# The filter's first layer: products in quarters of the array, and the decay split into a row table, scaled weights, a relu scale and a copy scale

## The chip, the core and the metric

The kernel runs on one core of one Trainium2 chip. The metric is the device time of one execution in microseconds. A profiled execution of the kernel before shows what each engine did; its rows are quoted below.

## What is computed

Three blocks follow one another on a sequence of 12480 positions with 128 channels, all in float32. The change touches only the filter of the first one, which is `h_filt` below.

```python
def _attn_ref(x, v, pos_emb, w1, w2):
    h_mlp = np.maximum(pos_emb @ w1, 0.0) @ w2          # (S,64) @ (64,64), then (S,64) @ (64,128)
    window = np.exp(-0.01 * np.arange(S))[:, None]
    h_filt = h_mlp * window
    u = x * v
    Uf = np.fft.rfft(u, n=2 * S, axis=1); Hf = np.fft.rfft(h_filt, n=2 * S, axis=0)
    y = np.fft.irfft(Uf * Hf[None], n=2 * S, axis=1)[:, :S, :]
    return x * y
# then relu(x @ w_in) ** 2 @ w_out, then elu(x @ w2_in) @ w2_out, with 2048 inner columns each
```

## The kernel before

The transform is a long one split into short ones. A position is 127*n + 63 plus or minus p, with n the row (R = 99 rows) and p = 0..63 the distance from a centre. `phase1` makes the first stage of both transforms, `phase2` the second stage, the product and the way back, and `phase3` the two wide layers, where nearly all of the time goes. The stages hand on through the same engines, so work of one stage starts once the last of the stage before has been issued and its inputs are there.

`phase1` runs in this order, which is also the order in each engine's queue. The kernel writes the order out by hand; TensorE (PE), VectorE (DVE), ScalarE (ACT) and GpSimd (POOL) each take their own instructions strictly in it.

1. `warm` issues six products of zeros on PE. SP, the queue of the loads, has issued the position embedding `post` (3.2 MB in six transfers, `load_pos`), then the tables `t1` and `tq`, then `x` and `v` by `load_xv(j)`, 512 KB each. ACT's queue has issued the table `wz` (the decay window `win` and `w1` twice on the diagonal of a 128x128 block).
2. Eight steps `zstep(s)` make the filter's first layer. In each, eight products (L293) multiply 128 rows of `post` (two sets of 64 features) by the block `w1`. The results lie in two PSUM tiles. The one of c=0 is brought out by ACT in eight instructions of 64 columns each (L302: relu, scaled with the decay of row and tap, which is a value of each partition). The one of c=1 is brought out by DVE in one instruction (L296: maximum with 0, times the window). Both go into a buffer `fb[s % 2]`, of which there are two. Then their sum is made by POOL and their difference by DVE (L309), and both go to `fold`. In the last step DVE makes both.
3. `warm` again, then 16 groups `s1` on the filter (L340): eight products each with the table `t1`, the stationary side being `fold`; ACT copies the result out. DVE meanwhile makes `u = x*v` and folds it (`ufold(j)`: L319, then L322 and L174; for six of the sixteen j twice the folding).
4. 32 groups `s1` on u, two for each j (L340, or L335 for the folded j, whose products each use a quarter of the array, 50 partitions by 64 columns). Their results go over the buffers of `v` (`xu`), which is why the first of them waits for the `ufold`s that read there. After the groups of j the loads of j+NX are issued and `ufold(j+NX)` follows.

`stile` hands out the PSUM tiles of all these steps in turn, four of them until call number NS1. NX is the count of `x` buffers (11), NV the count of separate `v` buffers (3); the `v` of j below 8 go to `xu`.

Of the kernel before, what the change touches and what calls it, by code (L numbers as in the profile page):

```python
# [10 lines left out]
F32 = mybir.dt.float32  # L11
# [3 lines left out]
AF = mybir.ActivationFunctionType  # L15
# [5 lines left out]
S = 12480  # L21
# [27 lines left out]
TOP = float(np.array(0x47EFFFFF, np.uint32).view(np.float32))  # L49
LO0 = 8  # L50
LAG1 = 2
NX = 11
NV = 3
NWARM = 6
NS1 = 55
MID = R // 2
RM = R - MID
FOLDED = (8, 9, 10, 12, 13, 14)
# [35 lines left out]
def tables():  # L94
    n1 = np.arange(R)
    k1 = np.arange(K1)
    k2 = np.arange(N2)
    pe, po = np.arange(CEN + 1), np.arange(1, CEN + 1)
    t = {}
    th = _angle((n1[:, None] - MID) * k1[None, :], N1)  # L100
    tq = np.stack([np.cos(th), -np.sin(th), -np.cos(th)], axis=1)[MID:].reshape(RM, 3 * K1)
    t["tq"] = np.zeros((128, 3 * K1))
    t["tq"][:RM] = t["tq"][64:64 + RM] = tq
    t["t1"] = np.stack([np.cos(th), -np.sin(th), -np.cos(th)], axis=2).reshape(R, 3 * K1)
    tf = np.zeros((2 * NP, N2, N2))
    k = k1[:, None, None] + N1 * k2[None, None, :]
    tf[:K1, :CEN + 1] = np.cos(_angle(pe[None, :, None] * k, L))
    tf[:K1, 0] = 0.5
    tf[:K1, CEN + 1:] = np.sin(_angle(po[None, :, None] * k, L))
    t["tf"] = np.zeros((NP, 128, 2 * N2))  # L110
    t["tf"][:, :N2] = tf.reshape(NP, 2, N2, N2).swapaxes(1, 2).reshape(NP, N2, 2 * N2)
    th = _angle(k2[:, None] * pe[None, :], N2)
    g = np.zeros((128, 128))
    g[:N2, 0] = 1.0
    g[:N2, 1:N2:2] = np.cos(th)[:, 1:]
    g[:N2, 2:N2:2] = np.sin(th)[:, 1:]
    t["g"] = g
    tl = _tiles()
    order = [s * p for p, s in tl[0][3]]
    at = np.concatenate(_rows()) - CEN - 2 * MID * N2  # L120
    c = np.where(k1 == 0, 1.0, 2.0)[:, None] / L
    th = _angle(k1[:, None] * at[None, :], L)
    re, im = c * np.cos(th), -c * np.sin(th)
    n = sum(tl[0][2])
    t["t3"] = np.stack([re[:, :n].reshape(K1, SIZES[0], -1), im[:, :n].reshape(K1, SIZES[0], -1)], axis=2)
    t["t3"] = t["t3"].reshape(K1, -1)
    t["ta"] = np.concatenate([re, im[:KA]])
    side = np.concatenate([np.full(nr, s) for _, _, nrs, rows in tl for (p, s), nr in zip(rows, nrs)])
    t["tb"] = np.concatenate([np.where(side == s, im[KA:], 0.0) for s in (1, -1)])
    sg = np.ones((128, 3))  # L130
    sg[:K1, 0] = sg[K1:, 1] = sg[K1 - KA:, 2] = -1.0
    t["sg"] = sg
    th = _angle((k[2 * PD:, 0, :, None, None] *
                 (np.array(order)[:, None] + N2 * (n1[None, :R - 1] - 2 * MID))[None, None]), L).reshape(KD, N2, -1)
    t["t4"] = np.zeros((128, 2 * th[:, 0].size))
    t["t4"][:N2] = (2.0 / L * np.stack([np.cos(th), -np.sin(th)], axis=1)).transpose(2, 0, 1, 3).reshape(N2, -1)
    pos = _taps().astype(np.float32)
    ok = (pos >= 0) & (pos < S)
    win = np.where(ok, np.exp(np.float32(-0.01) * np.where(ok, pos, np.float32(0.0))), 0.0)
    win = win.transpose(2, 0, 1).reshape(R, 8, 2, 4, 2).transpose(0, 1, 2, 4, 3).reshape(R, 128)  # L140
    t["wz"] = np.concatenate([win, np.zeros((128 - R, 128))])
    return {k: np.ascontiguousarray(a, dtype=np.float32) for k, a in t.items()}


# [19 lines left out]
class Build:  # L164
# [40 lines left out]
    def front(self):  # L205
        ctx0 = self.ctx
        with ExitStack() as self.ctx:
            self.mid = self.pool("mid")
            self.t1 = self.mid.tile([R, K1, 3], F32, name="t1")
            self.tq = self.mid.tile([128, 3, K1], F32, name="tq")  # L210
            self.psb = []
            self.right = ExitStack()
            self.x0pool = ctx0.enter_context(ExitStack())
            self.phase1()
            self.phase2()
            self.right.close()
        self.ctx = ctx0
# [7 lines left out]
    def phase1(self):  # L225
        nc, a = self.nc, self.a
        with ExitStack() as ctx1:
# [19 lines left out]
            self.xt = self.mid.tile([128, KTAIL * 2 * D], F32, name="xt")  # L247
            self.p2 = self.pool("p2")
            xvp = self.right.enter_context(self.tc.tile_pool(name="xv", bufs=1, side="right"))
            win, w1 = self.xt[:R, :128].rearrange("p (s c h n) -> p s c h n", s=8, c=2, h=2), self.xt[:, 128:256]  # L250
            fb = [self.xt[:R, o:o + 1024].rearrange("p (c h n e) -> p c h n e", c=2, h=2, e=E) for o in (256, 1280)]
            post = self.xr[:, :64 * R].rearrange("p (s w) -> p s w", s=8)
            fold = self.xu[2][:R, :2 * C1 * E].rearrange("p (o n e) -> p o n e", o=2, e=E)

# [4 lines left out]

            def load_xv(j):  # L260
                for i, (d, nm, n) in enumerate(((xs, "xc", NX), (vs, "vc", NV))):
                    if i and j < 8:
                        t = self.xu[j // 4][:, 1024 * (j % 4):1024 * (j % 4) + 1024]
                    else:
                        t = xvp.tile([128, 1024], F32, tag=nm, name=nm, bufs=n)
                    d[j] = t
                    nc.sync.dma_start(out=t, in_=a["xv"][j, i])
# [3 lines left out]
                for _ in range(n):  # L271
                    nc.tensor.matmul(ps[:, 0, :128], lhsT=self.zero, rhs=self.zero, start=True, stop=True)

            nc.scalar.dma_start(out=self.xt[:, :256], in_=a["wz"])
            self.copy(self.ebias[:, 2:3], self.zero[:, 0:1])
            for w in range(2):
                load_pos(0, 1, slice(4 * R * w, 4 * R * w + 4 * R))
            warm(NWARM)
            for b, e in ((1, 2), (2, 4), (4, 6), (6, 8)):
                load_pos(b, e)  # L280
            nc.sync.dma_start(out=self.t1.rearrange("p k a -> p (k a)"), in_=a["t1"])
            nc.sync.dma_start(out=self.tq.rearrange("p a k -> p (a k)"), in_=a["tq"])
            for j in range(8):
                load_xv(j)

            def zstep(s):
                f = fb[s % 2]
                for c in range(2):
                    ps = stile(2, 512)[:R, 0]
                    z = ps.rearrange("p (h n e) -> p h n e", h=2, e=E)  # L290
                    for q in range(4):
                        i = 4 * c + q
                        nc.tensor.matmul(ps[:, 128 * q:128 * q + 128], lhsT=post[:, s, i * R:i * R + R], rhs=w1,  # L293
                                         start=(q == 0), stop=(q == 3))
                    if c == 1:
                        nc.vector.scalar_tensor_tensor(  # L296
                            out=f[:, 1], in0=z, scalar=0.0,
                            in1=win[:, s, 1].unsqueeze(3).to_broadcast([R, 2, 4, E]), op0=ALU.max, op1=ALU.mult)
                        continue
                    for h in range(2):  # L300
                        for n in range(4):
                            nc.scalar.activation(out=f[:, 0, h, n], in_=z[:, h, n], func=AF.Relu,  # L302
                                                 scale=win[:, s, 0, h, n:n + 1])
                f = f.rearrange("p c h n e -> p c h (n e)")
                parts = [(nc.gpsimd, 0, slice(0, 2)), (nc.vector, 1, slice(0, 2))]
                if s == 7:
                    parts = [(nc.vector, 0, slice(0, 2)), (nc.vector, 1, slice(0, 2))]
                for eng, o, c in parts:
                    eng.tensor_tensor(out=fold[:, o, 8 * s:8 * s + 8].rearrange("p (c n) e -> p c (n e)", c=2)[:, c],  # L309
                                      in0=f[:, c, 0], in1=f[:, c, 1], op=(ALU.add, ALU.subtract)[o])  # L310

            for s in range(8):
                zstep(s)
# [8 lines left out]
                    nc.vector.tensor_tensor(out=o[:, :, 0], in0=i[:, :, 0], in1=i[:, :, 1], op=ALU.add)  # L322
                    self.sub(nc.vector, o[:, :, 1], i[:, :, 0], i[:, :, 1])

            def s1(i, fb, dst, w, last=None):
                ps = stile(2, 512)
                pv = ps[:, :, :4 * K1].rearrange("p b (c e) -> p b c e", e=2)
                halves = ((0, C1), (C1, N2))
# [8 lines left out]
                                                 start=(j == 0), stop=(j == 3))  # L337
                for j in range(4 if isinstance(fb, list) else 0):
                    for q, (b, e) in enumerate(halves):
                        nc.tensor.matmul(pv[b:e, j // 2, :, j % 2], lhsT=fb[j][q], rhs=self.t1[:, :, q:q + 2],  # L340
                                         start=(j % 2 == 0), stop=(j % 2 == 1))
                b = 0
                for o, n in dst:
                    o = o.rearrange("p (c d) -> p c d", d=w)[:N2, :, 4 * i:4 * i + 4]
                    o, z = o.rearrange("p c (b e) -> p c b e", e=2), pv[:N2, :, b:b + n].rearrange("p b c e -> p c b e")
                    b += n
                    if last and b == 2 * K1:
                        last(o, z)
                    else:
                        self.copy(o, z)  # L350

            for j in range(8, NX):
                load_xv(j)
# [1 line left out]
            for j in range(NX):  # L355
                ufold(j)
            for i in range(E // 4):
                s1(i, [(fold[:, 0, :, 4 * i + c], fold[:, 1, 1:, 4 * i + c]) for c in range(4)], [(self.xr, 2 * K1)], E)
            dst = [(t, n) for t, n in zip(self.xu + [self.xt], (32, 32, 64, 2 * KTAIL))]
            self.raw = {}  # L360
            for j in range(D // 8):
# [674 lines left out]
```

## Time and profile before

| | us |
|---|---|
| median of 3 runs | 1343.35 |
| lowest, highest | 1343.01, 1344.01 |
| profiled execution, its own time | 1345.65 |
| profiled execution, its span (first to last instruction) | 1343.9 |
| PE busy in the span | 1332.8 |

The page of the profile gives the span, the busy time of each engine and the chain of work that ended last. Beneath it lie views of any stretch: instructions in order of time, groups by line and shape, busy time by stretch, the waits. A row of the timeline reads: start, length, engine, line, operation, output<-input, shape, how many instructions were merged into it, and in brackets the idle time before it with what ended that. PE's products in float32 show two records each in the trace, and so do the loads of their weights.

### The profile page before, as it was taken

The page shows a single profiled execution, that of the slowest core. Times are in us where ns is not written, and L with a number is a line of the kernel's source. Part 1 is how long each engine was busy: PE and PEld are TensorE (multiplying, and loading weights), DVE is VectorE, ACT ScalarE, POOL GpSimd, SP SyncE. Part 2 cuts the span into 40 slices and gives each one's busy share as a digit, 9 for nine tenths or more (in the row PEclk, how much of TensorE's full clock was granted, in tenths as well). Part 3 has the DMA queues.
Part 4 walks back from the last instruction along what each step waited for, and adds up shares of the span by engine and source line. Part 5 has one row for each costly group of instructions (what it writes and reads, how often), then busy time and mean ns, then how long its engine had stood idle before and what let it go on. Part 6 is the DMA issues. An engine that isn't in the chain of part 4 may idle for free.

```text
span 1343.9 us, 19149 instructions
## 1 busy us (share of the span) xinstructions
PE 1332.8 (99%) x7150; PEld 1110.1 (83%) x7150; DVE 1182.5 (88%) x1210; ACT 1117.1 (83%) x1431; POOL 621.7 (46%) x364
## 2 busy tenths in 40 slices
PE   9999999999999999999999999999999999999998
PEld 9977778888888888888888888888888888888886
DVE  6969886889989898989899889989898989899897
ACT  6778775788988898889888888988898889888886
POOL 3038680545744454444444444444444445444432
PEclk9999999999999999999999999999999999999999
DMA  9746775301110111011001101110111011100000
GB/s 362 276 134 212 206 233 153 115 1 51 53 49 5 53 53 44 10 53 53 26 28 53 53 9 45 53 52 1 53 53 48 5 53 53 32 5 9 8 8 14
DMA packets 72443, 93.32 MB, mean 69 GB/s; under 512 B 5627, under 2 KB 62966, under 8 KB 72350
## 3 DMA queue, kind: packets, MB, share of 16 engines
q1 hardware_dynamic: 72062, 91.80, 21.9%
q8 instruction: 56, 0.92, 0.3%
q14 instruction: 37, 0.30, 0.1%
q10 hardware_dynamic: 288, 0.30, 0.1%
HBM read 73.72 MB, written 18.32 MB: 68 GB/s over the span
## 4 chain that ended last, share of the span: by engine, by line
PE 96%; DVE 2%; ACT 1%; issue 0%; DMA 0%; POOL 0%; SPq 0%; DVEq 0%; ACTq 0%
PE h L202 39%; PE y L202 38%; PE s L340 3%; PE v L559 3%; PE u L536 3%; PE h L677 2%; PE h L408 2%; PE h L681 2%; PE rt L395 1%; PE s L293 1%; DVE g L956 0%; DVE tn L942 0%; PE s L335 0%; DVE ex L872 0%; PE y L815 0%
## 5 line engine op out<-in xcount | busy, mean ns | idle before, releaser
L174 POOL TENSOR_TENSOR lo<-g,hi 128x1024 fp32r<-128x1024 f32 (+2 forms) x192 | 467.8, 2437 | 602.2 <-DVE tn L942 495.9
L202 PE MATMUL h<-xh,m 128*128 128x512 f32 (+3 forms) x1600 | 421.4, 385 | 3.4 <-DVE g L956 2.3
L202 PE MATMUL y<-hi,m 128*128 128x512 f32 (+2 forms) x1568 | 418.9, 389 | 0.0
L202 PEld LDWEIGHTS h<-xh,m 128*128 128x128 f32 x1600 | 298.6, 188 | 62.6 <-DVE g L956 3.4
L202 PEld LDWEIGHTS y<-hi,m 128*128 128x128 f32 x1568 | 290.0, 188 | 59.5 <-ACT ys L177 4.7
L942 DVE SCALAR_TENSOR_TENSOR tn<-ex,tn 128x1024 f32<-128x1024 f32 (+4 forms) x201 | 240.5, 1196 | 98.0 <-ACT ex L866 96.8
L865 ACT ACTIVATE tn<-h 128x1024 f32<-128x1024 f32 (+4 forms) x201 | 201.7, 1003 | 148.0 <-PE h L202 148.0
L174 DVE TENSOR_TENSOR lo<-ex,hi 128x1024 fp32r<-128x1024 f32 (+3 forms) x192 | 248.5, 1294 | 0.0
L956 DVE SCALAR_TENSOR_TENSOR g<-h,r 128x1024 f32<-128x1024 f32 (+3 forms) x200 | 238.4, 1192 | 9.2 <-ACT r L952 9.2
L202 PE MATMUL h<-xl,m 128*128 128x512 f32 (+3 forms) x800 | 242.2, 384 | 0.0
L202 PE MATMUL y<-lo,m 128*128 128x512 f32 (+2 forms) x784 | 239.8, 387 | 0.8 <-DVE lo L174 0.4
L872 DVE SCALAR_TENSOR_TENSOR ex<-tn,h 128x1024 f32<-128x1024 f32 (+4 forms) x201 | 237.2, 1180 | 1.5
L965 ACT ACTIVATE hi<-r 128x1024 fp32r<-128x1024 f32 (+3 forms) x200 | 209.8, 1049 | 0.5
L952 ACT ACTIVATE r<-h 128x1024 f32<-128x1024 f32 (+3 forms) x200 | 202.4, 1012 | 8.3 <-PE h L202 6.9
L177 ACT ACTIVATE hi<-ex 128x1024 fp32r<-128x1024 f32 (+2 forms) x192 | 203.9, 1062 | 1.6 <-DVE ex L872 1.5
L866 ACT ACTIVATE ex<-h 128x1024 f32<-128x1024 f32 (+4 forms) x201 | 199.8, 994 | 0.0
L202 PEld LDWEIGHTS y<-lo,m 128*128 128x128 f32 x784 | 146.7, 188 | 32.0 <-DVE lo L174 2.4
L202 PEld LDWEIGHTS h<-xl,m 128*128 128x128 f32 x800 | 149.6, 188 | 28.5
L551 POOL TENSOR_TENSOR pt<-pt 127x256 f32<-127x256 f32 x43 | 33.5, 779 | 82.0 <-DVE pt L548 81.9
L559 PE MATMUL v<-pt,g 127*128 127x512 f32 (+1 forms) x92 | 48.5, 612 | 0.0
L756 DVE SCALAR_TENSOR_TENSOR v<-z,sg 118x384 f32<-118x384 f32 (+3 forms) x75 | 43.0, 574 | 0.0
L548 DVE TENSOR_TENSOR pt<-u,hh 127x512 f32<-127x512 f32 (+1 forms) x46 | 31.2, 679 | 13.0 <-PE u L536 12.5
(93 smaller groups left out, 1059.0 us busy)
## 6 DMA issues: line engine op xcount, KB each, us to landing
Zd<-z SPq DMA_DIRECT2D x45, 256.0 KB
z<-Zd SPq DMA_DIRECT2D x48, 192.0 KB
xc<-in_xv_dram SPq DMA_DIRECT2D x16, 512.0 KB
z<-Zd SPq DMA_DIRECT2D x48, 136.5 KB
tb<-in_tf_dram SPq DMA_DIRECT2D x46, 127.0 KB
out_dram<-ys SPq DMA_DIRECT2D x22, 256.0 KB
m<-in_xv_dram SPq DMA_DIRECT2D x8, 512.0 KB
vc<-in_xv_dram SPq DMA_DIRECT2D x8, 512.0 KB
```

The source lines that it names most:

```text
L174: return eng.tensor_tensor(out=out, in0=a, in1=b, op=ALU.subtract)
L177: self.nc.scalar.activation(out=out, in_=in_, func=AF.Copy)
L202: self.nc.tensor.matmul(outs[b], lhsT=w[:, b, h], rhs=x[b], start=first and i in ((0,) if one else (0, 2)), stop=last and i in ((5,) if on ...
L559: nc.tensor.matmul(v, lhsT=self.g[:N2], rhs=pt.rearrange("p j r d -> p (j r d)"), start=True, stop=True)
L756: nc.vector.scalar_tensor_tensor(out=v[:k, i, q], in0=zi[:, :, 1], scalar=self.sg[:k, i:i + 1], in1=zi[:, :, 0], op0=ALU.mult, op1=ALU.add)
L865: nc.scalar.activation(out=e["tn"][:, b], in_=e["h"][:, b], func=AF.Tanh, scale=0.5)
L866: nc.scalar.activation(out=e["ex"][:, b], in_=e["h"][:, b], func=AF.Exp)
L872: nc.vector.scalar_tensor_tensor(out=e["g"][:, b], in0=e["em"][:, b], scalar=0.0, in1=e["h"][:, b], op0=ALU.min, op1=ALU.max)
L942: after = nc.vector.scalar_tensor_tensor(out=pa["em"][:, b], in0=pa["ex"][:, b], scalar=1.0, in1=pa["tn"][:, b], op0=ALU.add, op1=ALU.mult)
L952: nc.scalar.activation(out=f["r"], in_=f["h"], func=AF.Relu)
L956: nc.vector.scalar_tensor_tensor(out=f["g"], in0=f["h"], scalar=0.0, in1=f["r"], op0=ALU.max, op1=ALU.mult)
L965: nc.scalar.activation(out=f["hi"], in_=f["r"], func=AF.Square)
```

## The change

The first layer's products are cut into quarters. A step covers eight taps on both sides of the centre. `post` is laid out so that partitions 0 to 63 hold its first four taps and 64 to 127 its last four; each product takes 64 of these partitions, 64 (or the last 35) of the 99 rows, and 64 columns of weights. A step has 32 such products in place of eight, and its results fill both banks of one PSUM tile: z[:, 0] and z[:, 1] are the two sides, whose sum and difference are wanted. The decay exp(-0.01*pos) is split in four: over the rows n into a second table `tw` = `t1` times the row's decay, over the taps into eight copies of `w1`, each scaled (`ws`, made by DVE at the start by two instructions from `w1` and `near`), over the sides into a constant in ACT's relu, and over the groups of eight taps into `far`, a scale in ACT's copy of the filter's `s1`.

To bring out a step ACT makes one relu of z[:, 1] (99x512), and DVE makes sum and difference straight from PSUM: max(z[:, 0], 0) plus or minus that. In the steps 1, 3 and 5 (`ADDED`) ACT makes a relu of z[:, 0] as well, and POOL makes the difference from the two, so that DVE has only the sum. `post` is loaded in nine transfers, `tw` follows it, and `t1` and `tq` move behind the loads of j = 3. NX goes from 11 to 10 to make room for `tw`; the `v` of j = 7 goes to a separate buffer (NU = 7). NS1 goes down by the eight PSUM tiles that are no longer used.

```diff
-NX = 11
+NX = 10
 NV = 3
+NU = 7
+ADDED = (1, 3, 5)
+RATE = float(np.float32(0.01))
-NS1 = 55
+NS1 = 47
@@ tables
+    rate = np.exp(-RATE * N2 * np.arange(R))
+    t["tw"] = t["t1"] * rate[:, None]
+    near = np.exp(-RATE * np.array([1, -1])[:, None] * np.arange(8))
+    far = np.exp(-RATE * 8 * (np.arange(CEN + 1) // 8))
...
@@ phase1
-            win, w1 = self.xt[:R, :128].rearrange("p (s c h n) -> p s c h n", s=8, c=2, h=2), self.xt[:, 128:256]
-            fb = [self.xt[:R, o:o + 1024].rearrange("p (c h n e) -> p c h n e", c=2, h=2, e=E) for o in (256, 1280)]
+            w1, near, far = self.xt[:, :E], self.xt[:, E:E + 8], self.xt[:, E + 8:E + 9]
+            ws = self.xt[:, 128:640].rearrange("p (h q e) -> p h q e", h=2, e=E)
+            relu = [[self.xt[:R, o + 512 * h:o + 512 * h + 512].rearrange("p (b w) -> p b w", b=2)
+                     for h in range(2)] for o in (640, 1664)]
...
-                    if i and j < 8:
+                    if i and j < NU:
...
-            nc.scalar.dma_start(out=self.xt[:, :256], in_=a["wz"])
+            nc.scalar.dma_start(out=self.xt[:, :E + 9], in_=a["wz"])
             for w in range(2):
                 load_pos(0, 1, slice(4 * R * w, 4 * R * w + 4 * R))
             warm(NWARM)
-            for b, e in ((1, 2), (2, 4), (4, 6), (6, 8)):
-                load_pos(b, e)
+            for h in range(2):
+                nc.vector.tensor_tensor(out=ws[:, h], in0=w1.unsqueeze(1).to_broadcast([128, 4, E]),
+                                        in1=near[:, 4 * h:4 * h + 4].unsqueeze(2).to_broadcast([128, 4, E]), op=ALU.mult)
+            for s in range(1, 8):
+                load_pos(s, s + 1)
+            nc.sync.dma_start(out=self.tw.rearrange("p k a -> p (k a)"), in_=a["tw"])
+            for j in range(4):
+                load_xv(j)
             nc.sync.dma_start(out=self.t1.rearrange("p k a -> p (k a)"), in_=a["t1"])
             nc.sync.dma_start(out=self.tq.rearrange("p a k -> p (a k)"), in_=a["tq"])
-            for j in range(8):
+            for j in range(4, 8):
                 load_xv(j)
             def zstep(s):
...
+                z = stile(2, 512)[:R].rearrange("p b (h q e) -> p h b q e", h=2, e=E)
+                for h in range(2):
                     for q in range(4):
+                        i = (4 * (q // 2) + 2 * h + q % 2) * R
+                        for p in (slice(0, E), slice(E, 128)):
+                            for m in (slice(0, 64), slice(64, R)):
+                                nc.tensor.matmul(z[m, h, p.start // E, q], lhsT=post[p, s, i + m.start:i + m.stop],
+                                                 rhs=ws[p, h, q], start=(h + q == 0), stop=(h + q == 4))
+                z = z.rearrange("p h b q e -> p h b (q e)")
+                zr = relu[s % 2]
+                for h in (1, 0) if s in ADDED else (1,):
+                    nc.scalar.activation(out=zr[h], in_=z[:, h], func=AF.Relu,
+                                         scale=float(np.exp(16 * RATE * s)) if h else 1.0)
+                for o in range(2):
+                    dst = fold[:, o, 8 * s:8 * s + 8].rearrange("p (b q) e -> p b (q e)", b=2)
+                    op = (ALU.add, ALU.subtract)[o]
+                    if o and s in ADDED:
+                        nc.gpsimd.tensor_tensor(out=dst, in0=zr[0], in1=zr[1], op=op)
+                    else:
+                        nc.vector.scalar_tensor_tensor(out=dst, in0=z[:, 0], scalar=0.0, in1=zr[1],
+                                                       op0=ALU.max, op1=op)
@@ s1
-                        self.copy(o, z)
+                        nc.scalar.activation(out=o, in_=z, func=AF.Copy, scale=scale)
...
-                s1(i, [...], [(self.xr, 2 * K1)], E)
+                s1(i, [...], [(self.xr, 2 * K1)], E, t1=self.tw, scale=far[:N2])
```

## Rows read from the trace of the kernel before

**Rows 1.** The page's head: the span, and the chain that ended last by engine.

```profile
span 1343.9 us, 19149 instructions
PE 96%; DVE 2%; ACT 1%; issue 0%; DMA 0%; POOL 0%; SPq 0%; DVEq 0%; ACTq 0%
```

**Rows 2.** The chain in order of time, 19 to 63 us: start, length, what.

```profile
19.39 1.79 POOL m L309
...
21.89 0.55 PE s L340 x2
...
22.45 40.02 PE s L340 x509
```

**Rows 3.** Timeline of ACT, POOL and DVE in the filter's first layer.

```profile
5.97 1.75 ACT L302 ACTIVATE xt<-s,xt 99x64 f32<-99x64 f32 x8 [3.30 <-PE s L293]
...
8.22 3.63 POOL L309 TENSOR_TENSOR m<-xt 99x512 f32<-99x512 f32 x2 [7.78 <-DVE xt L296]
8.25 1.75 ACT L302 ACTIVATE xt<-s,xt 99x64 f32<-99x64 f32 x8 [0.53 <-PE s L293]
...
10.04 0.69 DVE L309 TENSOR_TENSOR m<-xt 99x512 f32<-99x512 f32 x1 [0.22 <-ACT xt L302]
10.29 9.95 ACT L302 ACTIVATE xt<-s,xt 99x64 f32<-99x64 f32 x44 [0.29 <-POOL m L309]
...
21.10 1.29 DVE L309 TENSOR_TENSOR m<-xt 99x512 f32<-99x512 f32 x2 [0.46 <-ACT xt L302]
```

**Rows 4.** Groups by line and shape, 0 to 22 us: busy us, mean ns | idle before.

```profile
L302 ACT ACTIVATE xt<-s,xt 99x64 f32<-99x64 f32 x64 | 14.0, 330 | 4.4 <-PE s L293 3.8 <-POOL m L309 0.3
L309 POOL TENSOR_TENSOR m<-xt 99x512 f32<-99x512 f32 x7 | 12.4, 1776 | 8.4 <-DVE xt L296 7.8 <-ACT xt L302 0.3
...
L296 DVE SCALAR_TENSOR_TENSOR xt<-s,xt 99x512 f32<-99x512 f32 x8 | 5.5, 691 | 7.5 <-PE s L293 7.4
```

**Rows 5.** The same view, 62 to 120 us: quarter products, an ACT copy from PSUM.

```profile
L335 PE MATMUL s<-tq,xc 50*64 50x91 f32 x192 | 8.9, 241 | 0.6 <-issue 0.3 <-ACT xt L177 0.3
...
L177 ACT ACTIVATE z<-v 128x512 f32<-128x512 f32 x13 | 7.7, 594 | 1.4 <-PE v L559 1.3
```

**Rows 6.** Timeline of POOL and DVE, 103 to 116 us.

```profile
103.89 0.69 DVE L548 TENSOR_TENSOR pt<-u,hh 127x512 f32<-127x512 f32 x1
103.90 1.29 POOL L174 TENSOR_TENSOR m<-wf,m 128x512 fp32r<-128x512 f32 x1 [0.22 <-ACT m L177]
...
114.81 1.11 DVE L466 SCALAR_TENSOR_TENSOR wf<-raw,we 128x512 uint32<-128x512 uint32 x1
115.33 1.73 POOL L174 TENSOR_TENSOR m<-wf,m 128x512 fp32r<-128x512 f32 x1
```

**Rows 7.** PE's timeline from 62 us: the first quarter products of u.

```profile
62.38 1.81 PE L335 MATMUL s<-tq,xc 50*64 50x91 f32 x80
```

**Rows 8.** Busy time by stretch, L293 alone: length, PE (records), PEld, granted clock, DMA.

```profile
3.91:5.91 2.00, 2.00 (x9) 2.00 (x10) 1.00 0.83 203
...
6.91:8.91 2.00, 2.00 (x20) 1.96 (x18) 1.00 1.01 401
9.20:19.20 10.00, 10.00 (x92) 10.00 (x93) 1.00 1.04 393
```

**Rows 9.** Timeline of SP, the queue that issues the loads.

```profile
7.03 0.33 SPq L267 DMA_DIRECT2D xc<-in_xv_dram  x1
...
13.29 0.33 SPq L267 DMA_DIRECT2D m<-in_xv_dram  x1
...
34.95 1.76 SPq L422 DMA_DIRECT2D w<-in_w_dram  x2
```

**Rows 10.** Waits of SP's queue, 0 to 80 us: us in total, times, longest.

```profile
SPq L267 <- DMA xr<-in_post_dram: 6.2, 4, 2.0
```

**Rows 11.** Timeline of DVE: the last `ufold` of an early load, and a late copy.

```profile
39.59 1.23 DVE L319 TENSOR_TENSOR m<-xc,m 128x1024 f32<-128x1024 f32 x1
...
71.95 0.38 DVE L348 COPY xt<-s 127x216 f32<-127x216 f32 x1 [1.98 <-ACT m L177]
```

More of the change, by code (lines that the diff above doesn't have):

```diff
@@ L136, in tables @@
     t["t4"][:N2] = (2.0 / L * np.stack([np.cos(th), -np.sin(th)], axis=1)).transpose(2, 0, 1, 3).reshape(N2, -1)
[L137 to L141, printed above, removed]
+    rate = np.exp(-RATE * N2 * np.arange(R))
+    t["tw"] = t["t1"] * rate[:, None]
+    near = np.exp(-RATE * np.array([1, -1])[:, None] * np.arange(8))
+    far = np.exp(-RATE * 8 * (np.arange(CEN + 1) // 8))
+    t["wz"] = np.concatenate([near.reshape(2, 2, 4).swapaxes(0, 1).reshape(2, 1, 8).repeat(E, 1).reshape(128, 8),
+                              np.concatenate([far, far[1:], [0.0]])[:, None]], axis=1)
     return {k: np.ascontiguousarray(a, dtype=np.float32) for k, a in t.items()}
@@ L208, in front @@
             self.mid = self.pool("mid")
-            self.t1 = self.mid.tile([R, K1, 3], F32, name="t1")
+            self.t1, self.tw = (self.mid.tile([R, K1, 3], F32, name=nm) for nm in ("t1", "tw"))
             self.tq = self.mid.tile([128, 3, K1], F32, name="tq")
@@ L281, in phase1 @@
+            for j in range(4):
+                load_xv(j)
             nc.sync.dma_start(out=self.t1.rearrange("p k a -> p (k a)"), in_=a["t1"])
             nc.sync.dma_start(out=self.tq.rearrange("p a k -> p (a k)"), in_=a["tq"])
-            for j in range(8):
+            for j in range(4, 8):
                 load_xv(j)
             def zstep(s):
[L287 to L290, printed above, removed]
+                z = stile(2, 512)[:R].rearrange("p b (h q e) -> p h b q e", h=2, e=E)
+                for h in range(2):
@@ L291, in zstep @@
                     for q in range(4):
[L292 to L307, printed above, removed]
@@ L308, in zstep @@
-                for eng, o, c in parts:
-                    eng.tensor_tensor(out=fold[:, o, 8 * s:8 * s + 8].rearrange("p (c n) e -> p c (n e)", c=2)[:, c],
-                                      in0=f[:, c, 0], in1=f[:, c, 1], op=(ALU.add, ALU.subtract)[o])
+                        i = (4 * (q // 2) + 2 * h + q % 2) * R
[3 more added lines that the diff above has]
+                                                 rhs=ws[p, h, q], start=(h + q == 0), stop=(h + q == 4))
@@ L323, in ufold, with s1 @@
                     self.sub(nc.vector, o[:, :, 1], i[:, :, 0], i[:, :, 1])
-            def s1(i, fb, dst, w, last=None):
+            def s1(i, fb, dst, w, last=None, t1=self.t1, scale=1.0):
                 ps = stile(2, 512)
@@ L339, in s1 @@
                     for q, (b, e) in enumerate(halves):
-                        nc.tensor.matmul(pv[b:e, j // 2, :, j % 2], lhsT=fb[j][q], rhs=self.t1[:, :, q:q + 2],
+                        nc.tensor.matmul(pv[b:e, j // 2, :, j % 2], lhsT=fb[j][q], rhs=t1[:, :, q:q + 2],
                                          start=(j % 2 == 0), stop=(j % 2 == 1))
@@ L357, in phase1 @@
             for i in range(E // 4):
-                s1(i, [(fold[:, 0, :, 4 * i + c], fold[:, 1, 1:, 4 * i + c]) for c in range(4)], [(self.xr, 2 * K1)], E)
+                s1(i, [(fold[:, 0, :, 4 * i + c], fold[:, 1, 1:, 4 * i + c]) for c in range(4)], [(self.xr, 2 * K1)], E,
+                   t1=self.tw, scale=far[:N2])
             dst = [(t, n) for t, n in zip(self.xu + [self.xt], (32, 32, 64, 2 * KTAIL))]
@@ L1011 @@
     xv = rows
-    post = _take(pos_emb, _taps()).reshape(8, 2, 2, 2, 2, R, E).transpose(0, 3, 6, 1, 4, 2, 5).reshape(8, 128, -1)
+    post = _take(pos_emb, _taps()).reshape(8, 2, 2, 2, 2, R, E).transpose(0, 1, 6, 2, 4, 3, 5).reshape(8, 128, -1)
     arrays = {
@@ L1019 @@
     arrays.update(tables())
-    w = np.zeros((128, 128), np.float32)
-    w[:E, :E] = w[E:, E:] = w1
-    arrays["wz"] = np.concatenate([arrays["wz"], w], axis=1)
+    arrays["wz"] = np.concatenate([np.concatenate([w1, w1]), arrays["wz"]], axis=1)
     arrays = {k: np.ascontiguousarray(t) for k, t in arrays.items()}
```

## The prediction

> **What bounds the kernel now.** I read the page's head first, then the chain of waits in order of time, then the timeline of the stretch that the change touches, then single prices. The head says that the chain lies on PE for 96% [rows 1]. So an edit in the filter's first layer, which fills only the first 22 us, can pay in one way: by letting the long run of PE's work behind it begin earlier. The chain shows where that run begins: POOL's last sum starts at 19.39 and takes 1.79, PE takes up the first `s1` at 21.89, and from 22.45 PE goes on for 40.02 us without a gap [rows 2]. The point to move is DVE's last difference, which ends at 21.10 + 1.29 = 22.39 [rows 3]. What it gains is the time that the kernel gains, unless something behind it comes late.
>
> What sets 22.39? The timeline shows three engines in step [rows 3]: ACT starts its third step at 10.29, 0.29 us after POOL's first sum ended (8.22 + 1.78 = 10.00), because the two buffers `fb` must be free. POOL makes seven sums of 1.776 us, 12.4 in all, and ACT 64 relus in 14.0 [rows 4]. PE's eight products of a step take 16 records of 10.00/92 = 0.109 us, 1.74 us [rows 8]. So PE, ACT and POOL each need about 1.75 us a step, and relief of one alone would give nothing. The change relieves all three.
>
> **The change part by part.** *Products.* 32 of them are 64 records a step. The nearest row is the quarter products of u: 80 records in 1.81 us, the last being 0.241 long itself, so (1.81 - 0.24)/79 = 19.9 ns from start to start [rows 5, 7]. These have 91 columns, the new ones 64, so by columns it would be 14.0 ns. I take 19.9, as nothing in the trace shows a shorter pace: 64 x 19.9 = 1.27 us a step. Bounds: 14.0, and 28 to 40 if PE is at its lower clock level, since the first products show 9 or 10 records in 2.00 us against 20 later, twice the time, though the granted clock reads 1.00 in both stretches [rows 8]. That is 1.2 against 2.4 GHz; the rise falls between 5.91 and 6.91, after PE had worked on zeros and then on the first step.
>
> *Start.* The first step now waits for DVE to scale `w1`, two instructions of 256 columns. A DVE instruction of 512 takes 0.691 and one of 216 takes 0.38 [rows 4, 11], so 0.43 each. The first products then start near 4.5 in place of 3.9 to 4.0, which is covered: the second step can't begin before its part of `post` has landed. SP's issue at 7.03 is the first of four that waited for `post`, 6.2 us in total [rows 9, 10]; I read it as the landing of the second part. `wz` is 94 KB shorter and was ahead of it, 0.2 us at 401 GB/s [rows 8]. So 6.8, bounds 6.5 and 7.0. The second step's products end at 6.8 + 1.27 + 0.24 = 8.3, and ACT starts on them at 8.35. Three more issues of SP cost 0.33 each [rows 9], covered since its next issues wait for landings anyway. The last `post` has landed by 13.29 [rows 9]; its step is not wanted before 15.
>
> *The round of the odd steps.* The steps 1, 3, 5 and 7 share one relu buffer, since it is chosen by s % 2. ACT may refill it only when POOL has read it. So a round is: two relus on ACT, POOL's difference, and back. A 512-column copy from PSUM takes 0.594 [rows 5]. Back-to-back instructions overlap: eight of 0.330 fill 1.75, so (1.75 - 0.33)/7 = 0.20 apart, 0.13 less than their length [rows 3, 4]. Two relus: 1.06. ACT to POOL: ACT's eight end at 10.00, DVE starts at 10.04 and POOL's second sum at 8.22 + 3.63 - 1.78 = 10.07 [rows 3], so 0.07. POOL's difference: 1.776 by the row of the same shape [rows 4], or 1.29 by an instruction of 512 columns elsewhere [rows 6]. Rows 6 say which: 1.29 while DVE reads one operand from PSUM (L548), 1.73 when DVE began first on one whose operands both lie in SBUF (L466). In the old step DVE's L309 was of the second kind, in the new one DVE reads z from PSUM. I take 1.29. Back to ACT 0.29 [rows 3]. The round is 1.06 + 0.07 + 1.29 + 0.29 = 2.71 us for two steps, against 3.5 now. PE needs 2 x 1.27 = 2.55 in it, DVE 1.29 + 0.69, so the round is just the longest.
>
> The Trainium skill (SBUF — State Buffer, section "SBUF: two separate sides") says the same of POOL and DVE: they share a pair of ports, held for a whole instruction by whichever starts first, against a DVE instruction with two SBUF inputs. Rows 6 bear it out (1.29 and 1.73).
>
> *Sum.* ACT takes step 1 at 8.35; three rounds later, 8.35 + 8.13 = 16.48, step 7. Its relu 0.59, 0.04 to DVE, and DVE's two 1.29 [rows 3]: 18.40. Against 22.39 that is 3.99 us earlier.
>
> *What must keep up.* PE's 16 filter groups keep their length: same columns with `tw`, and a copy with a scale on ACT, which has room (it is not in the 40.02 us of the chain [rows 2]); I cost it at nothing, and would pay only beyond 1.25 us a group. `ufold` is DVE's and starts with its last difference. Its loads don't come earlier, since all of them stand behind 3.2 MB of `post`: SP issues each load when one some eight issues earlier has landed, and I read the two issues from 34.95 (1.76 in all) as the landing of those of j = 7, by 36.4 [rows 9]. DVE took them at 39.59 [rows 11]: 3.2 us in hand. Shifted by 4.0, DVE waits 0.8 there. PE doesn't feel it: it needs the buffers of `v`, of which j = 7 is now apart, and u of j = 7 only 17 us into its groups on u. NX = 10 makes the load of j = 10 wait for the first u groups; DVE may lose another half microsecond. The margin is at the end of the stage: DVE's copy at 71.95 had idled 1.98 before it [rows 11], and 0.8 + 0.5 is less. Moving `t1` and `tq` behind j = 3 is free (first needed after the filter's groups), and `tw`, 0.1 MB, takes 0.3 us after `post`, landing near 13.6. Everything behind shifts with PE.
>
> So the span 1343.9 becomes 1339.9, the profiled execution's own 1345.65 becomes 1341.7, and the median 1343.35, on which I forecast, **1339.4**.
>
> **The rivals.**
> 1. *Rounds don't bind* (the wait for POOL is shorter than I read, and columns set PE's pace): DVE is next, 13 instructions of about 0.65 and two of 0.43 behind a first result near 7: about 17.2, gain 5.1, 1338.2.
> 2. *POOL stays at 1.776.* For it: the same shape, seven times with that mean. Against it: rows 6. 3 x 0.49 = 1.5 less gain: 1340.8.
> 3. *PE's pace is longer than 19.9.* The row's products use 50 partitions and the new ones 64; were the pace to go by that, 25.5 ns, PE would set the end: 6.8 + 7 x 64 x 0.0255 = 18.2, then 0.24 + 0.05 + 0.63 + 1.29: 20.4, gain 2.0, 1341.3. Against it: the pace is already that of 91 columns. The Trainium skill (TensorE: Matmul & The Clock Gate, section "Wait — 56ns, not 53.3ns?") has a rule of this sort: matmuls never start closer than about 25 ns, however few columns. By it the gain would be 2.2 and the time 1341.2; the records at 19.9 ns [rows 7] lie below it, and the measurement decides.
> 4. *PE idles and its clock falls.* PE is done with the last step and `warm` some 2 us before `s1` can begin; now it idles from 21.18 to 21.89 [rows 2]. If the level then drops, each filter group costs 1.25 us more (40.02/32 is one group). Two groups: gain 1.5, 1341.8. No row shows PE idle that long, so this stays open.
> 5. *Slower: quarter products don't bring the clock up.* PE stays at 1.2 GHz through the layer, at 40 ns a record: 6.8 + 7 x 64 x 0.040 = 24.7, end 26.9, 4.5 us later than now: 1347.9. It decides from a pace of 29.9 ns on (then the end is 22.4 as now). Against it: quarter products of u kept 19.9 ns [rows 7], though after long full work. That the quarters do not run at once at all (half of 0.109 a record, 54 ns, 33 us, some 1354) is the same place with a higher price, and the same row speaks against it.
>
> **How the numbers follow.** Forecast 0.57 (its own range 1338.6 to 1340.9), rival 1 0.07, rival 2 0.12, rival 3 0.08, rival 4 0.10, rival 5 0.06. A measurement of this kernel tells about 0.2%, 2.7 us, from no change; faster is then below 1340.7, slower above 1346.0. Faster: 0.53 of the forecast, 0.07 of rival 1 and 0.02 of rival 2, 0.62. Slower: 0.06. The rest, 0.32, is the same. The range goes from rival 1, 1338.2, to 1343.0, which takes in rivals 2 and 3, most of 4, and the first round at PE's low level (up to 1.3 us); left out are rival 5 and ends of the others.
>
> **What would show it.** In the profile after: ACT's relu of step 1 starting at 8.35 and those of 3, 5, 7 about 2.7 apart, each 0.29 behind POOL; POOL's three at 1.29; 64 records a step in 1.3 us; DVE's last difference near 18.4 and PE's unbroken run from 18.5 for 40 us; `ufold`s waiting for loads at j = 5 to 7 and PE not. It is wrong if POOL's instructions take 1.78, if ACT's odd relus are released by PE rather than POOL, if the first filter groups take twice their time, or if PE's run on u has new gaps.

## The result, and the profile after

The changed kernel takes 1350.82 us (median of 5 runs, 1349.43 to 1352.98) against 1343.85 of the kernel before: 7.0 us longer. The ratio is 1.0054, 95% interval 1.0044 to 1.0065. I had forecast 1339.4 and a range up to 1343.0. The profiled execution took 1351.04, its span is 1349.2.

The chain of the changed kernel in order of time (start, length, what), where [rows 2] answer for the kernel before:

```profile
6.46 2.61 PE s L305 x139
9.07 3.35 issue
12.42 3.09 PE s L305 x124
15.51 3.25 issue
18.76 3.68 PE s L305 x126
22.44 2.46 issue
24.90 1.55 PE s L305 x47
26.45 2.86 PE s L278 x12
29.31 40.39 PE s L349 x507
```

PE's long run begins at 29.31 in place of 22.45, 6.9 us late, and that is the loss. (Between the two profiled spans only 5.3 are left, mainly because the kernel before ran 3.4 us at half clock from 225.4 on in that execution.) Ahead of the run stand three pieces in which PE did nothing and waited for nothing that the profile knows, 9.1 us together.

PE's timeline shows where they fall. The first step is a group of 64 records, and then:

```profile
6.46 2.61 PE L305 MATMUL s<-xt,xr 64*64 64x64 f32 x146 [0.23 <-DMA xr<-in_post_dram]
12.42 3.09 PE L305 MATMUL s<-xt,xr 64*35 64x64 f32 x127 [3.35 <-issue]
18.76 3.68 PE L305 MATMUL s<-xt,xr 64*64 64x64 f32 x127 [3.25 <-issue]
24.90 1.55 PE L305 MATMUL s<-xt,xr 64*64 64x64 f32 x48 [2.46 <-issue]
```

A step is 64 records. The stops come after 210, 337 and 464, so 18, 17 and 16 into a step: no buffer, no landing and no PSUM tile changes there. Between them lie 127 records each time, that is 127 pairs of a weight load and a product, 254 instructions. The DMA queues of 9 to 26 us (kind: packets, MB, share) have a row for instructions, first in the changed kernel, then in the one before:

```profile
q8 instruction: 3, 0.05, 1.2%
```

```profile
q8 instruction: 1, 0.02, 0.4%
```

A packet has 16 KB, so some 64 bytes for each of 254 instructions. PE is waiting for its own program. The trace times these packets: in the changed kernel they land at 11.00, 17.27 and 23.64, and PE goes on 1.42, 1.49 and 1.26 us later. The eight stops of this kind in the layer in e2, e7 and e10 below end in the same way, 1.3 to 1.6 us after a packet has landed. The starts of the blocks are 6.34 and 6.14 us apart, however fast PE runs them.

And the clock follows. Busy time by stretch (length, PE, PEld, DVE, ACT, POOL, granted clock, DMA share, GB/s):

```profile
9.00:12.40 3.40, 0.07 (x2) 0.00 (x0) 1.69 (x3) 0.36 (x1) 1.12 (x1) 1.00 1.05 391
12.40:15.50 3.10, 3.08 (x127) 2.92 (x127) 0.69 (x1) 1.40 (x3) 0.86 (x1) 0.62 1.03 385
24.90:29.30 4.40, 4.40 (x62) 4.06 (x61) 2.12 (x3) 0.60 (x1) 0.00 (x0) 0.50 1.03 407
```

After the first gap, at 13.17, the granted clock goes to 0.50, 1.2 GHz, and stays there until the filter's groups have begun. The zeros behind the last step then take 2.86 us and end 0.8 after DVE's last difference (27.18 + 1.29 = 28.47).

The Trainium skill (Runtime: NRT & Kernel Launch, section "Instruction fetch mechanics") says that an engine's instructions are refilled in blocks of 16 KB, 256 instructions, while it works on those before, and that this is mostly hidden. The packets agree with the size of the block; hidden it is not here, with 9.1 us of gaps.

### The profile page after: what moved, and what is told of

Its sections match the earlier page's. It is cut to its first block, busy times and chain, and to the rows that moved or that the text cites. A ratio compares the mean times of both kernels' runs of the same rounds, so it can differ in the third digit from the quotient of the medians.

```text
span 1349.2 us, 19844 instructions
## 1 busy us (share of the span) xinstructions
PE 1329.5 (99%) x7534; PEld 1104.3 (82%) x7534; DVE 1180.3 (87%) x1208; ACT 1110.8 (82%) x1378; POOL 612.9 (45%) x360
## 4 chain that ended last, share of the span: by engine, by line
PE 95%; DVE 1%; DMA 1%; issue 1%; ACT 1%; SPq 0%; POOL 0%; DVEq 0%; POOLq 0%
PE h L206 38%; PE y L206 38%; PE s L349 3%; PE v L569 3%; PE u L546 3%; PE h L687 2%; PE h L418 2%; PE h L691 2%; PE rt L405 1%; PE s L305 1%; DMA tb<-in_tb_dram 1%; DVE tn L952 0%; PE y L825 0%; PE s L344 0%; DMA xr<-in_post_dram 0%
```

## The experiments

Three theories stood against each other. A: PE runs out of instructions, which come late while loads run. B: a wait for a buffer or PSUM that the profile does not name. C: quarters of the array stall by themselves.

### e1: half the instructions, same waits

```diff
-for m in (slice(0, 64), slice(64, R)):
-    nc.tensor.matmul(z[m, h, p.start // E, q], lhsT=post[p, s, i + m.start:i + m.stop], ...)
+nc.tensor.matmul(z[:, h, p.start // E, q], lhsT=post[p, s, i:i + R], ...)
```

> The changed kernel with products of 64 partitions by all 99 rows: 16 a step in place of 32, so 32 pairs of weight load and product, with the same waits, buffers, loads and evictions. Theory A (PE runs out of instructions: in the changed kernel it stops inside a step, each time after 127 pairs, and the next pairs come 6.1 to 6.3 us after the ones before, while the DMA engines are full): a block of 127 pairs now lasts four steps, so 49 ns a pair is all that can be had; PE's own pace is 46 to 59 ns (weights of 99 columns, by the 127 columns of line 408), so the gaps shrink to 0 to 0.5 us each, DVE's last difference falls to 19.5 to 21, and the time is 1340 to 1343. Theory B (a wait on relu buffers or PSUM that the profile calls issue): nothing that waits has changed, so three gaps near 3 us and about 1350 stay. Theory C (quarters of the array stall by themselves): the gaps go as in A.

Measured: 1349.95, ratio 1.0037 (1.0021 to 1.0053). Eight of its ten times lie between 1349.75 and 1350.75, the others are 1340.67 and 1344.64. Its chain:

```profile
4.26 21.60 PE s L304 x256
25.86 2.86 PE s L278 x12
28.71 40.40 PE s L348 x512
```

Not one gap is left: 256 pairs in one piece, with every wait as it was. That speaks against B, though PE is so slow here that a short wait could hide; e4 has no gap at twice the pace, and with it B falls. The time missed A's expectation by 7 us for another reason: 84 ns a pair, where I had counted 46 to 59, and the zeros behind at 2.86. That is PE at 1.2 GHz through the whole layer, although the views print a granted clock of 1.00. The trace holds no record of the clock ahead of 29.65 us, and the views print 1.00 where there is none. Of the two short executions no trace was kept; a clock that rose early would fit them, but that is not shown. Of the clock, e4 below.

### e2: no loads beside the steps

```diff
 for s in range(8):
     zstep(s)
+note = self.dram.tile([R, E], F32, name="note")
+nc.sync.dma_start(out=note, in_=fold[:, 0, 8 * 7])   # behind it, SP issues x, v, t1 and tq
```

> The changed kernel with the loads of x and v (and the tables t1, tq) held back on their queue until DVE has made the sum of the last step; products stay quarters. From the landing of the last part of the position embedding, near 12 us, the DMA engines are then idle until the steps are done. Theory A: PE's gaps behind 12 us go (under 1 us), the one from 9 shrinks to 3 or less, the last difference falls from 28.5 to 17 to 20. The loads then start some 12 us late, so the filter's groups end about when the first seven products u are there (near 39), and the time is 1340 to 1344. Theories B and C: the gaps are still three of 2.5 to 3.4 us, the last difference stays near 28, and with the late loads the time is 1353 or more.

Measured: 1352.78, ratio 1.0079 (1.0061 to 1.0097). PE's timeline, and the DMA queues from 13 to 21 us:

```profile
6.86 2.74 PE L300 MATMUL s<-xt,xr 64*64 64x64 f32 x146 [1.63 <-DMA xr<-in_post_dram]
13.09 2.65 PE L300 MATMUL s<-xt,xr 64*35 64x64 f32 x127 [3.48 <-issue]
16.84 4.88 PE L300 MATMUL s<-xt,xr 64*64 64x64 f32 x175 [1.09 <-issue]
```

```profile
q8 instruction: 2, 0.03, 1.7%
```

The first gap is as long as ever (I had expected 3 or less): the position embedding was still landing. The second, with two instruction packets as all that moves, is 1.09 in place of 3.25, and the third is gone, 175 pairs running over a block's border. The two blocks start 3.75 us apart. (The clock is at 0.50 from 14.37 to 21.19, so PE also takes longer over a block than at full clock; but the changed kernel, at 0.50 too, still had 2.46 at this place.) C falls: whether quarters stall depends on the loads. The packets show where the time goes. When PE goes on after a stop, the next packet starts 3.6 to 3.9 us later beside loads (nine cases: the changed kernel, e7 and e10), and 1.2 and 1.4 us later here, with the engines idle. The packet's own 0.9 to 1.3 us and the 1.3 to 1.6 until PE goes on are the same in both.

The total was wrong, and with 1352.78 it does not tell A from B and C, as the late loads cost more than I allowed. They hold up `ufold` and at the end of the stage PE itself, by 5.9 us in the profiled execution, which is the longest of the four (1357.81, the others 1352.07 to 1352.88):

```profile
PE s L347 <- DVE xt L360: 5.9, 1, 5.9
```

### e3: the rest of the change, with products over the whole array

```diff
-for p in (slice(0, E), slice(E, 128)):
-    for m in (slice(0, 64), slice(64, R)):
-        nc.tensor.matmul(z[m, h, p.start // E, q], lhsT=post[p, s, ...], rhs=ws[p, h, q], ...)
+nc.tensor.matmul(ps[:, h, 128 * q:128 * q + 128], lhsT=post[:, s, i:i + R], rhs=ws[:, h, q], ...)
```

The scaled weights lie on the two diagonal blocks, the taps are laid out to match.

> The changed kernel with eight products a step over the whole array, as in the kernel before (128 partitions, 99 rows, 128 columns, scaled weights on the two diagonal blocks), all else of the change kept: the new evictions, loads and tables. Theory A: 16 pairs a step at 0.109 us, a block of 127 pairs lasts 14 us, no gap; PE sets the pace at 1.74 a step and the last difference comes at 20.5 to 21.8: 1341.5 to 1343.5. Theory B: the waits are the same, the gaps stay and the time is near 1350. Theory C: as A. If it lies above 1344, something else in the change costs too.

Measured: 1344.47, ratio 1.0005 (0.9995 to 1.0014), no difference, and 1 us above what A expected. Its chain:

```profile
4.59 14.42 PE s L306 x128
...
21.15 39.92 PE s L350 x510
...
65.38 1.39 issue
```

No gap in the layer, and PE's run begins 1.3 us earlier than before: evictions, tables and loads of the change do no harm there. But 1.1 of it goes at 65.4, in the quarter products of u, where the kernel before has 0.31 of "issue" and this one 1.39. With NX = 10 the last loads of u run later, into the stretch where PE uses up its instructions fastest.

### e4: halves, with the clock up beforehand

```diff
-            warm(NWARM)
+            warm(2 * NWARM)      # ahead of the first step, in e1
```

> The halves (64 partitions by 99 rows, 16 products a step) with twelve in place of six products of zeros before the first step. In the run with halves PE had no gap but took 21.6 us for its 256 pairs, 84 ns a pair, where 99 weight columns at 2.4 GHz would be 41; the granted clock read 1.00, but the pace is that of 1.2 GHz through the whole layer, and the two lots of zeros took 2.9 us each, twice their 1.4. Theory D (work in halves does not raise the clock by itself, but keeps it once it is up): the longer run of whole-array zeros, to 6.9 us, raises it before the first step; then 42 to 49 ns a pair, steps from 6.9 to 18 or 20, last difference 20 to 22, 1340.5 to 1343. Theory E (work in halves lets it fall, or the pace is something else, such as PSUM): still 84 ns a pair, first step 2.6 us later, 1350 to 1353.

Measured: 1341.55 (1340.92 to 1342.15), ratio 0.9988 (0.9978 to 0.9997): shorter than before. The chain:

```profile
1.05 4.76 PE s L278 x24
5.81 11.35 PE s L304 x256
...
19.32 40.03 PE s L348 x508
...
63.41 1.04 issue
```

44 ns a pair in place of 84: D holds, E falls. Products of halves keep the clock once it is up, but in e1's profile did not raise it in 21 us. No gap shows at a border of blocks: 127 pairs now last 5.6 us. That is a little less than the 6.1 to 6.3 us between blocks in the changed kernel. At the one border in this layer that follows a whole block of halves, the packet had landed 1.7 us before PE got there, so there was little to spare.

### e5: whole array, eleven x buffers

```diff
-NX = 10
+NX = 11
```

> The whole-array version of the change with eleven x buffers again. In the whole-array run PE began its long run at 21.15, 1.3 us earlier than in the kernel before, but lost 1.1 of it at 65.4, where it had a gap of 1.39 us (0.31 before) in the quarter products of u while the loads of u were still coming. Theory A (instructions of PE come late while loads run): with one more x buffer the last loads run earlier, the gap at 65 goes back to 0.3 to 0.6, and the time is about 1 us under that of the whole-array run, 1342 to 1343.5. If buffers do not matter, it is the same as that run, near 1344.5.

```profile
4.69 16.25 PE s L306 x128
...
23.08 39.92 PE s L350 x510
...
66.62 1.22 PE s L345 x31
```

Measured: 1343.58, ratio 1.0000 (0.9990 to 1.0010). The gap in the products of u is gone, as A says. The time says little: in this profile the layer itself took 16.25 against 14.42 in e3, its first steps at the low pace for longer (the clock's first record at 1.00 stands at 8.87, in e3 at 4.21).

### e6: more instructions with almost no work

```diff
+for _ in range(3 if q < 3 else 0):
+    nc.tensor.matmul(ps[:1, h, 128 * q:128 * q + 1], lhsT=zero[:, :1], rhs=zero[:, :1], start=False, stop=False)
```

> The whole-array version with three products of one weight column by one column of zeros behind each of the first three products of a bank: 18 more pairs a step, 34 in place of 16, which add nothing to the result and move almost no data. Theory A: at 34 pairs a step a block of 127 pairs is used up in 3.7 steps; PE's own work is 1.74 us and 18 times at most 25 ns, 2.2 us a step, so a block lasts at least 8 us, more than the 6.2 it takes to come: no gap, PE ends near 22 and the time is 1344 to 1347. Gaps that are put down to nothing here would speak for another cause than the supply of instructions.

Measured: 1377.85, one run. PE's timeline:

```profile
5.21 0.46 PE L306 MATMUL s<-xt,xr 128*99 128x128 f32 x2
5.60 0.29 PE L309 MATMUL s<-zero 128*1 128x1 f32 x6
5.83 0.46 PE L306 MATMUL s<-xt,xr 128*99 128x128 f32 x2
```

A miss by 30 us, and no test of A. The expectation also miscounted: 18 products of two pairs each (the x6 above is three products) make 52 pairs a step, not 34. A product with its three tiny ones takes 0.62 us, where it takes 0.22 alone, and 0.9 once the clock has fallen: the tiny ones, or the change of shape around them, cost far more than the 25 ns that I had allowed. PE never gets near the rate at which instructions come.

### e7: quarters, with the clock up beforehand

The edit is that of e4, made in the changed kernel.

> The changed kernel (quarters) with twelve products of zeros before the first step in place of six. Theory A with the clock as a consequence: the clock is up before the first step, but PE still runs out after a block of 127 pairs, twice or three times for 2 to 4 us, falls back to 1.2 GHz there, and the last difference comes at 26 to 30: 1347 to 1352. Theory F (the low clock is the cause and the gaps its result): with the clock up early the gaps go and the time is under 1343.

Measured: 1352.33, one run. PE's timeline:

```profile
6.47 3.14 PE L305 MATMUL s<-xt,xr 64*64 64x64 f32 x198
13.13 3.61 PE L305 MATMUL s<-xt,xr 64*35 64x64 f32 x127 [3.52 <-issue]
19.29 3.06 PE L305 MATMUL s<-xt,xr 64*64 64x64 f32 x127 [2.55 <-issue]
25.60 1.92 PE L305 MATMUL s<-xt,xr 64*64 64x64 f32 x60 [3.25 <-issue]
```

At full pace from the first step (3.14/198, 16 ns) PE meets the same three gaps, with blocks 6.16 and 6.31 apart. There are 12 more pairs ahead of the steps, and the first stop comes 12 pairs earlier in them, after 198 in place of 210: the border is counted in instructions. F falls; the low clock is a result of the gaps.

### e8 and e9: the better version, and whether zeros alone make it

e8 is e4 with NX = 11. e9 is the kernel before with `warm(2 * NWARM)` ahead of its first step.

> Halves with twelve products of zeros ahead, and eleven x buffers again. In the run with ten, PE's long run began 3.1 us earlier than in the kernel before, and 1.0 was lost in a gap at 63.4 us in the quarter products of u, while the last loads of u were still coming. Theory A (instructions come late while loads run): with eleven buffers the gap is 0.3 or none, and 2.4 to 3.2 us are left of the gain: 1340.3 to 1341.2 where the kernel before takes 1343.5. If the gap stays, 1341.5.

> The kernel before with twelve products of zeros ahead of the first step in place of six, nothing else. Is the gain of the halves version one of the zeros alone? Theory D: the kernel before raises its clock in its first two steps by itself (16 records at half speed, 1.7 us lost); with the longer zeros the first step starts 1.8 us later at full speed, so nothing is won: 1343 to 1344.5, last difference at 22 to 23.5. If the zeros are the whole gain: 1341.5.

e8: 1341.11 (1340.33 to 1342.25), ratio 0.9984 (0.9975 to 0.9993), 2.0 us shorter than the kernel before on that chip and 9.2 than the changed one. e9: 1344.25, ratio 1.0008 (0.9999 to 1.0016), no gain. First e8's chain, then e9's:

```profile
5.61 11.35 PE s L304 x256
...
19.12 39.92 PE s L348 x510
...
63.11 0.13 issue
```

```profile
22.97 40.06 PE s L340 x506
```

The gap near 63 is 0.13, where e4 had 1.04, and the run begins 3.3 us earlier than in [rows 2].

### e10: the changed kernel again, on the chip of e8 and e9

> The changed kernel once more, on the chip of the other two, so that all are compared with the same runs of the kernel before. Theory A: again blocks of 127 pairs 6.1 to 6.4 us apart, two or three gaps of 2.4 to 3.6 us, last difference at 27 to 30, 1349 to 1352.

Measured: 1350.35, ratio 1.0054 (1.0040 to 1.0068). PE's timeline:

```profile
12.25 3.06 PE L305 MATMUL s<-xt,xr 64*35 64x64 f32 x127 [2.95 <-issue]
18.32 3.68 PE L305 MATMUL s<-xt,xr 64*64 64x64 f32 x127 [3.00 <-issue]
24.45 1.55 PE L305 MATMUL s<-xt,xr 64*64 64x64 f32 x48 [2.46 <-issue]
```

## Why the prediction was wrong, step by step

**The small steps held.** Timeline of the changed kernel, where [rows 3] answer:

```profile
3.78 0.76 DVE L286 TENSOR_TENSOR xt<-xt 128x256 f32<-128x256 f32 x2 [2.77 <-DMA xt<-in_wz_dram]
7.69 1.67 ACT L310 ACTIVATE xt<-s 99x512 f32<-99x512 f32 x3 [0.78 <-PE s L305]
8.86 1.27 POOL L316 TENSOR_TENSOR m<-xt 99x512 f32<-99x512 f32 x1 [8.41 <-ACT xt L310]
13.48 1.08 ACT L310 ACTIVATE xt<-s 99x512 f32<-99x512 f32 x2 [4.12 <-PE s L305]
27.18 1.29 DVE L318 SCALAR_TENSOR_TENSOR m<-s,xt 99x512 f32<-99x512 f32 x2 [3.14 <-ACT xt L310]
```

ACT takes step 1 at 7.69 (8.35 foretold; PE's second step began at 6.46, not 6.8), two relus last 1.08 (1.06), POOL's difference 1.27 (1.29; not the 1.78 of rival 2), DVE's pair 1.29. PE's pace within a block was 2.61/146 = 17.9 ns, under the 19.9 that I took, so rival 3 was no danger either. One sign of being wrong did come: ACT's relus waited for PE, 17.0 us in five waits, and never for POOL, so the rounds did not set the pace. And rival 1's sum does not come out as written: 7 + 13 x 0.65 + 2 x 0.43 is 16.3, not 17.2; only the low end of the range rests on it.

**The step that failed is the price of the products:** "64 x 19.9 = 1.27 us a step". It prices what PE does with its instructions and takes their coming for granted, at nothing. A block of 127 pairs comes every 6.1 to 6.3 us while the loads run, 49 ns a pair, 3.1 us a step: more than the 1.74 of the kernel before. From the first product (4.26) to the last (26.38) the 512 records took 43 ns each. The prediction's own sum for rival 5 has its turning point at 29.9 ns; with 43.2 it gives 6.8 + 7 x 64 x 0.0432 + 2.21 = 28.4 for the last difference, and 28.47 was measured. That says only that the rest of the sum closes, as the 43.2 comes from the same run. The slower side was there, but with the clock as its only mechanism and a chance of 0.06; that its 1347.9 comes nearer to the measured time than the forecast is luck, as its mechanism is another.

**Why the rows did not warn me.** My row for the pace [rows 7] is 80 records long, less than one block, in a stretch with hardly any loads. Behind it, out of the window that I quoted in [rows 2], the chain of the kernel before has two pieces that say it:

```profile
66.09 0.69 PE s L335 x21
66.78 0.31 issue
67.09 0.53 PE s L335 x11
```

Quarter products, cut in the middle of a group, with nothing waited for. I had read "issue" as noise. The trace has an instruction packet landing at 65.58, 1.5 us before PE goes on at 67.09. e3, e4 and e5 show the same place as 1.39, 1.04 and none, by how late the loads run.

**The clock.** Rival 4 (PE idles and its clock falls) did come, in the gaps and not where I had put it. By itself it cost some 1.9 us, an estimate: 0.7 in the last 48 pairs (1.55 us, where 17.9 ns a pair gives 0.86), 0.8 in the zeros that end after DVE's last difference, and 0.4 in the long run (40.39 against 40.02). Within the earlier blocks the slower pace lay under the wait for the next block. Rival 5's claim, that products in parts of the array do not bring the clock up, was seen for halves in e1's profile. Quarters ran at 18 ns a pair from 6.46 on, and in e2 the clock rose while PE had run nothing but quarters since 16.84 (same columns as above):

```profile
16.90:21.10 4.20, 4.20 (x150) 4.02 (x153) 1.40 (x3) 1.68 (x3) 1.27 (x1) 0.50 0.01 4
21.20:21.60 0.40, 0.40 (x33) 0.38 (x25) 0.40 (x2) 0.00 (x0) 0.00 (x0) 1.00 0.14 41
```

Why halves and quarters differ in this is open.

**Not tested:** whether the round of the odd steps (2.71 us for two) binds. In e4 and e8 PE's halves take 2.8 for two steps and hide it. Why the packet starts some 2.5 us later while loads run is also open: standing in line behind the loads' packets would fit, but no run tests it, and in the kernel before and e1, where PE does not stop in the layer, packets start 1.2 to 1.8 us after the border beside the same loads.

## What to carry to other kernels

Count the instructions of PE, not only its columns. Cutting a product in pieces pays only while a block of 254 instructions lasts at least about as long as the next takes to come, here some 6 us beside loads. With the same zeros and buffers, 16 products a step took 1341.55 us (e4) and 32 took 1352.33 (e7, one run), although the array needs longer for the 16 (1.4 us a step against 1.0 to 1.2). An "issue" piece in the middle of a group of equal products, with an instruction packet landing just before its end, is the sign.

## What the runs showed of the hardware that was not expected

- PE's instructions come in blocks of 127 pairs. Where PE is waiting for them, their starts are 6.1 to 6.3 us apart while the DMA engines are full and 3.75 us (one interval) while they are idle (e2). PE goes on 1.3 to 1.6 us after the packet has landed.
- Halves of 64 by 99 ran all of 21.6 us at 84 ns a pair (e1) and at 44 ns after a longer run of whole-array zeros (e4); the views print a granted clock of 1.00 in both. The first record of the clock stands at 29.65 us in e1 and at 4.88 in e4, and ahead of it the column does not tell the level; the pace does.
- Three products of one column between whole ones turned 0.22 us a product into 0.62 (e6).
